# Reading two DRAM-bounced tiles by rows of 16 or 32 partitions instead of by columns of 96, with the opening's requests reordered

## The chip, the cores and the metric

The kernel runs on one core of a Trainium2 chip. The metric is the device time of one launch in microseconds, as the median of several executions. A profiled execution of the same program gives the trace; its times are counted from the first instruction. "Span" is the time from the first to the last instruction in that trace, and the launch's own time is a little longer than the span.

The engines are named as the profile does: PE (matrix multiplies), PEld (weight loads for PE), DVE (vector), ACT (scalar), POOL (GpSimd) and SP (which here only issues DMA requests). SPq is SP's queue of requests.

## The reference, cut to what matters

Eight sequences of 3008 tokens with 256 channels go through a spectral layer, and the result through a two-layer expert with ELU:

```
X  = rfft(x, axis=1)                       # x: [8, 3008, 256]
Yr = Xr @ w_r - Xi @ w_i + b_r             # 256 x 256 weights
Yi = Xr @ w_i + Xi @ w_r + b_i
Yr, Yi = soft threshold by 0.01
y  = irfft(Yr + i Yi, n=3008)              # [8, 3008, 256]
h  = y @ moe_w_in                          # 256 x 2048
g  = where(h > 0, h, exp(min(h, 0)) - 1)
out = g @ moe_w_out                        # 2048 x 256
```

## The kernel before, in words

**The transform.** 3008 is 47 times 64, and each transform is done in two matrix steps with a trip through DRAM between them, because the second step contracts over another index than the first. For one batch the units are:

- A (6 units, `unit_A`): the transform over 64 samples. Each unit multiplies four of 24 column groups of the loaded input by the table `M1`, copies the result to SBUF as `A`, and writes it to the DRAM tile `DA` of shape [24 (j), 128, 256].
- Z: `load_Z` reads `DA` back with another split of its indices. The partitions of `Z` are (j, half, real or imaginary), 96 in all; the free dimension has 32 columns (s) of 256 channels, 16 KB for each partition in bf16.
- X (8 units, `unit_X`): the transform over 47, one small matmul for each column s, contracting over all 96 partitions of `Z`. Unit u uses columns 8(u//2) to 8(u//2)+7.
- M (12 groups, `unit_M` or in the opening `first_M`): the 256 x 256 complex weights, bias and soft threshold.
- B (6 units, `unit_B`): the inverse transform over 64, written to the DRAM tile `DB` of shape [24 (k), 128, 256].
- Bs: `load_Bs` reads `DB` back with 96 partitions (k, real or imaginary, half) and 32 columns, as `Z` is read.
- Y (8 units, `unit_Y`): the inverse transform over 47, contracting over all 96 partitions of `Bs`; unit u uses columns 8(u//2) to 8(u//2)+7.

**The expert.** All tokens are cut into blocks of 512, each block into 8 steps of 256 hidden columns. `front` multiplies by the scaled input weights and starts the exponential, `elu` and `finish_elu` complete it, and `back` multiplies by the output weights two steps later. One batch is 47 such steps, about 2.3 us each.

**What sets the order.** The program is written out by hand (`manual_schedule`): each engine executes its instructions in the order of the program text, and a DMA request waits on the queue of the engine that issues it, with everything that stands behind it. SP issues nearly all requests: writes of `DA` and `DB`, reads of `Z` and `Bs`, the weights and the output. POOL issues the reads of x and of the output weights. From batch 1 on, the transform of the next batch is spread over the expert steps of the current one by `plan` (f0: units ahead of the step's `front`; f1: requests after it). Batch 0 has nothing to hide behind: its transform is the opening, about 57 us, in which `idle_pe(n)` puts n matmuls without use into PE's queue to keep it running.

**The opening, in order.** Tables on DVE, ACT and POOL; six A units with a `DA` write each (line 155); the requests for w_r and w_i (518, 519); four reads of `Z`, eight columns each (164); 40 idle matmuls (562); X; M and B interleaved, with a `DB` write after each B (260); two reads of `Bs` (271); the six A units of batch 1 (each followed by two idle matmuls) with two more reads of `Bs` among them; then Y and the expert steps. The reads of `Z` and `Bs` can only start once all six writes have landed, since each column has parts of all of them; the first X unit needs only the first read of `Z`, the first Y unit only the first read of `Bs`.

Of the kernel before, what the change touches and what calls it, by code (L numbers as in the profile page):

```python
# [29 lines left out]
def kernel(  # L30
# [46 lines left out]
    dram = ctx.enter_context(tc.tile_pool(name="dram", bufs=2, space=bass.MemoryType.DRAM))  # L77
    zp = ctx.enter_context(tc.tile_pool(name="zp", bufs=1))
    wk2 = ctx.enter_context(tc.tile_pool(name="wk2", bufs=2))
    wk3 = ctx.enter_context(tc.tile_pool(name="wk3", bufs=3))  # L80
    wk4 = ctx.enter_context(tc.tile_pool(name="wk4", bufs=4))
    xtp = ctx.enter_context(tc.tile_pool(name="xtp", bufs=1))
# [46 lines left out]
    def unit_A(b, u, alone=False, on_dve=False, ahead=False):  # L129
        ci, uu = u // 2, u % 2  # L130
        if uu == 0:
            if ahead and ci > 0:
                A_of[b, ci] = late3.tile([P, 8, D], BF16, name="A", tag="gT")
            elif alone:
                A_of[b, ci] = wk4.tile([P, 8, D], BF16, name="A", tag="Bs")
# [5 lines left out]
        dav = DA_of[b].rearrange("j p d -> p j d")  # L141
# [6 lines left out]
        evac(  # L148
            A[:, 4 * uu : 4 * uu + 4, :].rearrange("p n d -> p (n d)"),
            ps[:].rearrange("p a b -> p (a b)"), on_dve,  # L150
        )
        j0 = 8 * ci
        if alone:
            j0 += 4 * uu
            nc.sync.dma_start(dav[:, j0 : j0 + 4, :], A[:, 4 * uu : 4 * uu + 4, :])
        elif uu == 1:
            nc.sync.dma_start(dav[:, j0 : j0 + 8, :], A[:])

    def load_Z(b, s0, s1):

        if b not in Z_of:
            Z_of[b] = zp.tile([2 * NR, NS, D], BF16, name="Z", tag="Z")
        dv = DA_of[b].rearrange("j (h c s) d -> (j h c) s d", h=2, c=2)
        nc.sync.dma_start(Z_of[b][:, s0:s1, :], dv[:, s0:s1, :])

# [100 lines left out]

    def load_Bs(b, w):

        Bs = wk4.tile([4 * K1, 8, D], BF16, name="Bs", tag="Bs")
        dv = DB_of[b].rearrange("k (c h m) d -> (k c h) m d", c=2, h=2)  # L270
        nc.sync.dma_start(Bs[:], dv[:, 8 * w : 8 * w + 8, :])
        Bs_of[b, w] = Bs

    def unit_Y(b, u, alone=False, on_dve=False):
        w, dt = u // 2, u % 2
        if u == 0:
            yT_of[b] = late2.tile([P, 2, S], BF16, name="yT", tag="yT")
        yT, Bs = yT_of[b], Bs_of[b, w]
        ps = unit_ps("yps", alone)
        psv = ps[:].rearrange("p a (k j) -> p (a k) j", j=P)  # L280
        for j in range(8):
            nc.tensor.matmul(  # L282
                psv[:, j, 0 : 2 * N1], lhsT=Bs[:, j, dt * P : dt * P + P], rhs=M4[:],
                start=True, stop=True,
            )
# [9 lines left out]
    def idle_pe(n):  # L295

        for _ in range(n):
            nc.tensor.matmul(ips[:], lhsT=busy[:, 0:P], rhs=busy[:], start=True, stop=True)

    brow, rest = (wk3.tile([P, 2 * D], F32, name="yb", tag="yb") for _ in range(2))  # L300
    nc.vector.memset(brow[:], 0.0)
    for o, bv in ((0, b_r), (D, b_i)):
        for k in range(3):
            nc.sync.dma_start(
                brow[32 * k : 32 * k + 1, o : o + D],
                bass.AP(tensor=bv.tensor, offset=bv.offset, ap=[[0, 1], [1, D]]),
            )
    idle_pe(9)
    xts = []
    for ci in range(3):  # L310
        xt = constp.tile([P, 8, D], F32R, name=f"xt{ci}")
        xts.append(xt)
    with tc.tile_pool(name="stagep", bufs=1) as stagep:
# [202 lines left out]
        signs(0)  # L516
        fA(5)
        nc.sync.dma_start(w_r_f[:], w_r.rearrange("(c p) e -> p c e", p=P))
# [42 lines left out]
        )  # L561
        idle_pe(40)

# [9 lines left out]
    def load_w_in(q):  # L573
        if q < 3:
# [9 lines left out]

    def gate(src):

        t = gatep.tile([P, 1], F32, name="gate", tag="gate")
        nc.gpsimd.tensor_copy(t[0 : src.shape[0], :], src)


    def fB(v, on_dve=False):
        unit_B(0, v, alone=True, on_dve=on_dve)

    load_w_in(0)
    gate(Z_of[0][:, 8, 0:1])
    for ci in range(3):
        load_x(1, ci)
    load_w_out(0)
    nc.vector.tensor_scalar(w3[:], v3[:], CMAGIC, -CMAGIC, ALU.add, ALU.add)
    nc.vector.tensor_tensor(w3[:], v3[:], w3[:], ALU.subtract)  # L600
    nc.scalar.copy(bias_p[:], brow[:])
    nc.vector.tensor_tensor(rest[:], brow[:], bias_p[:], ALU.subtract)
    for u in range(8):
        unit_X(0, u, alone=True, on_dve=u in (1, 4, 7))
        if u == 1:
            nc.scalar.activation(a3[:], w3[:], AF.Abs)
            nc.vector.tensor_copy(bias_p[32:64], rest[32:64])
            nc.vector.tensor_copy(bias_p[64:P], rest[64:P])
            nc.vector.tensor_tensor(rest[64:P], rest[64:P], bias_p[64:P], ALU.subtract)
            nc.vector.tensor_copy(bias_p[64:P], rest[64:P])  # L610
        idle_pe(1)
    for o, src, sc, bi in ((1, w3, TURN, 0.0), (0, a3, -TURN, hpi[:])):
# [12 lines left out]
    first_M(1, 0, False)  # L625
    nc.scalar.activation(r4[:], v4[:], AF.Sin, bias=0.0, scale=TURN)
    nc.scalar.activation(dume[:], busy[:, 0:1], AF.Exp, scale=0.0)
# [24 lines left out]
    load_Bs(0, 0)  # L652
    load_Bs(0, 1)

# [6 lines left out]

    scale_w_in(0, True)
    for u in range(6):
        unit_A(1, u, on_dve=bool(u % 2), ahead=True)
        if u == 1:
            scale_w_in(1, True)
            for w in (2, 3):
                load_Bs(0, w)
            gate(Bs_of[0, 2][:, 0, 0:1])
            load_w_out(1)  # L670
            load_w_in(3)
# [128 lines left out]
    def plan(b):  # L800
# [18 lines left out]
        for t, u in enumerate(seq, lead):  # L819
# [7 lines left out]
            else:  # L827
                f0[t].append(put(u[0], n1, *u[1:]))
            if u == ("A", 1):
                f1[t] += [(load_Bs, (n1, w)) for w in range(4)]  # L830
            if u == ("A", 5) and n2 < B:
                f1[t] += [(load_Z, (n2, s0, s1)) for s0, s1 in ((0, 8), (8, NS))]
        if b == 0:
            f1[3].append((scale_w_in, (3, True, 0)))
            f1[4].append((scale_w_in, (3, True, 1)))
            f1[xs[0]].append((lambda: gate(Z_of[1][:, 16, 0:1]), ()))
        if n2 < B:
# [61 lines left out]
```

## Time and profile before

| | |
|---|---|
| median of 3 runs | 912.49 us (911.72 to 914.93) |
| the profiled execution's own time | 911.36 us |
| its span | 909.6 us |
| PE busy | 893.2 us (98%) |
| DVE, ACT, POOL busy | 79%, 77%, 35% of the span |
| bytes moved by DMA | 106.24 MB, 117 GB/s on average |

The share of PE is an average. From about 60 us on PE is continuously fed; the opening is where PE's work is partly idle matmuls and waits. A line of the timeline gives start and length in us, the engine, the line of the code, the operation and, in brackets, the idle time before it and what ended it. A line of the windows gives a stretch, the busy time of each engine with the number of instructions, and at its end the clock granted to PE (1.00 is full), the busy share of the 16 DMA engines and the rate in GB/s.

### The profile page before, as it was taken

What the parts mean: (1) busy time and instruction counts of PE and PEld (TensorE: products, weight loads), DVE (VectorE), ACT (ScalarE), POOL (GpSimd) and SP (SyncE); (2) the same over time, 40 slices, a digit from 0 to 9 for tenths busy, and PEclk for the clock granted to TensorE, in tenths of its full rate; (3) what the DMA queues carried; (4) which work ended last, traced back from release to release, by engine and by line L of the source; (5) the groups of instructions that cost most, each with busy time, mean ns of one, the idle gap of its engine ahead of it and who ended that gap; (6) DMA issues with size and microseconds to landing.
All of it is one profiled execution on the core that took longest, in us unless ns stands there. A gap on an engine that the chain in (4) does not pass through costs nothing.

```text
span 909.6 us, 17270 instructions
## 1 busy us (share of the span) xinstructions
PE 893.2 (98%) x6721; PEld 652.3 (72%) x6721; DVE 717.5 (79%) x891; ACT 696.8 (77%) x850; POOL 314.9 (35%) x438
## 2 busy tenths in 40 slices
PE   8989999999999999999999999999999999999997
PEld 3447667876688667886678766787667866777775
DVE  8669778887788778897788877888778877778776
ACT  6768788777878778787787888778887877767664
POOL 6701540333321441405404153033332134443664
PEclk9999999999999999999999999999999999999999
DMA  8997116721283215732166032752228111231011
GB/s 270 309 269 228 47 48 186 209 70 47 77 241 124 71 47 143 190 109 85 56 201 194 24 99 59 217 161 72 69 72 230 30 42 47 82 82 48 24 48 46
DMA packets 90670, 106.24 MB, mean 117 GB/s; under 512 B 5270, under 2 KB 81308, under 8 KB 87228
## 3 DMA queue, kind: packets, MB, share of 16 engines
q1 hardware_dynamic: 84332, 77.62, 30.6%
q0 software_dynamic: 5968, 27.26, 9.1%
q8 instruction: 52, 0.85, 0.4%
q10 hardware_dynamic: 288, 0.26, 0.1%
q14 instruction: 30, 0.25, 0.1%
HBM read 55.32 MB, written 49.81 MB: 116 GB/s over the span
## 4 chain that ended last, share of the span: by engine, by line
PE 85%; DVE 5%; ACT 3%; DMA 3%; issue 2%; POOL 1%; SPq 1%; DVEq 0%; ACTq 0%; POOLq 0%
PE ps_o L773 34%; PE hps L715 34%; PE mps L192 9%; PE yps L282 2%; PE bps L244 2%; PE xps L175 2%; PE aps L144 2%; DMA Bs<-DB 2%; DVE gT L742 1%; DVE Et L754 1%; ACT Et L729 1%; ACT Et L726 1%; DMA xt<-in_x_dram 1%; DVE osb L784 1%; ACT Bz L257 1%
## 5 line engine op out<-in xcount | busy, mean ns | idle before, releaser
L773 PE MATMUL ps_o<-w_out_r,gT 128*128 128x256 f32 x3008 | 477.0, 301 | 0.2 <-DVE gT L740 0.2
L773 PEld LDWEIGHTS ps_o<-w_out_r,gT 128*128 128x128 f32 x3008 | 403.4, 189 | 50.3 <-DVE osb L784 1.3
L715 PE MATMUL hps<-yT,w_in_s 128*128 128x512 bf16 (+4 forms) x1728 | 389.9, 353 | 2.5 <-DVE gT L742 1.2
L740 DVE SCALAR_TENSOR_TENSOR gT<-Et,hps 128x512 fp32r<-128x512 f32 (+1 forms) x272 | 222.8, 848 | 75.3 <-POOL Et L752 38.2
L742 DVE SCALAR_TENSOR_TENSOR gT<-hps,Et 128x1024 fp32r<-128x1024 f32 x198 | 242.2, 1223 | 16.5 <-PE ps_o L773 1.0
L715 PEld LDWEIGHTS <-w_in_s 128*128 128x128 bf16 x1728 | 141.6, 98 | 129.4 <-issue 23.0
L729 ACT ACTIVATE Et<-hps 128x1024 f32<-128x1024 f32 x198 | 204.0, 1030 | 13.2 <-PE hps L715 6.7
L752 POOL TENSOR_SCALAR Et<-Et 128x512 f32<-128x512 f32 x187 | 111.4, 615 | 222.9 <-ACT Et L724 222.9
L754 DVE TENSOR_SCALAR Et<-Et 128x1024 f32<-128x1024 f32 x198 | 137.0, 692 | 48.0 <-ACT Et L729 40.1
L210 POOL TENSOR_SCALAR clip<-yb 128x512 f32<-128x512 f32 x84 | 51.7, 615 | 316.0 <-DVE yb L202 278.6
L724 ACT ACTIVATE Et<-hps 128x512 f32<-128x512 f32 x188 | 102.1, 595 | 63.9 <-PE hps L715 63.9
L726 ACT ACTIVATE Et<-hps 128x1024 f32<-128x1024 f32 x84 | 86.3, 1027 | 71.5 <-PE hps L715 71.0
L211 POOL TENSOR_TENSOR Y<-yb,clip 128x512 bf16<-128x512 f32 x84 | 107.2, 1276 | 7.0
L727 ACT ACTIVATE Et<-Et 128x1024 f32<-128x1024 f32 x84 | 88.8, 1058 | 2.7
L202 DVE TENSOR_TENSOR yb<-mps,bias_bc 128x512 f32<-128x512 f32 x89 | 61.4, 689 | 35.4 <-PE mps L192 28.6
L127 ACT CAST XT<-xps 128x768 bf16<-128x768 f32 x61 | 48.8, 800 | 15.8 <-PE xps L175 15.8
L127 ACT CAST yT<-yps 128x752 bf16<-128x752 f32 x63 | 49.7, 788 | 14.2 <-PE yps L282 14.1
L192 PE MATMUL mps<-wcat_r,XT 128*128 128x512 bf16 x192 | 58.2, 384 | 0.8 <-ACT Bz L257 0.3
L127 ACT CAST A<-aps 128x1024 bf16<-128x1024 f32 x45 | 45.6, 1014 | 15.3 <-PE aps L144 13.8
L192 PE MATMUL mps<-wcat_s,XT 128*128 128x512 bf16 x192 | 57.1, 379 | 0.0
L192 PEld LDWEIGHTS <-XT 128*128 128x128 bf16 x384 | 30.8, 98 | 29.6 <-DVE XT L125 0.6
L257 ACT CAST Bz<-bps 128x1024 bf16<-128x1024 f32 x46 | 46.0, 1000 | 2.5 <-PE bps L244 2.5
(110 smaller groups left out, 412.9 us busy)
## 6 DMA issues: line engine op xcount, KB each, us to landing
xt<-in_x_dram POOLq DMA_DIRECT2D x21, 1024.0 KB, 7.1
out_dram<-osb SPq DMA_DIRECT2D x158, 128.0 KB
Bs<-DB SPq DMA_DIRECT2D x32, 384.0 KB
DA<-A SPq DMA_DIRECT2D x21, 512.0 KB
DB<-Bz SPq DMA_DIRECT2D x21, 512.0 KB
Z<-DA SPq DMA_DIRECT2D x7, 1152.0 KB
Z<-DA SPq DMA_DIRECT2D x11, 384.0 KB
xt<-in_x_dram POOLq DMA_DIRECT2D x6, 512.0 KB, 5.9
```

The lines of the kernel that those rows point to most:

```text
L127: nc.scalar.copy(dst, src)
L192: nc.tensor.matmul(ps, lhsT=XT[:, dt, c, o : o + P], rhs=wm[:, dt, :], start=(not biased and m == 0 and dt == 0), stop=(m == 1 and dt == 1),)
L211: nc.gpsimd.tensor_tensor(Y_of[b, q][:, i, :], yb, clip[:], ALU.subtract)
L715: nc.tensor.matmul(hps[:, s, c0:c1], lhsT=w_in_s[:, dt, ft * P : ft * P + P], rhs=yT_of[b][:, dt, t0 : t0 + c1 - c0], start=(dt == 0), sto ...
L724: nc.scalar.activation(E_[:, s], hps[:, s], AF.Exp)
L726: nc.scalar.activation(E_, hps[:], AF.Relu, scale=-1.0)
L729: nc.scalar.activation(E_, hps[:], AF.Exp)
L740: nc.vector.scalar_tensor_tensor(o, e, -1.0, h, ALU.add, ALU.max)
L742: nc.vector.scalar_tensor_tensor(o, h, 0.0, e, ALU.max, ALU.add)
L752: eng.tensor_scalar(E_[:, s], E_[:, s], 1.0, 0.0, ALU.min, ALU.max)
L754: nc.vector.tensor_scalar(E_, E_, 1.0, -1.0, ALU.min, ALU.add)
L773: nc.tensor.matmul(po[q][:, i_ % 2, :], lhsT=gT[:, s, i_ * P : i_ * P + P], rhs=w_out_r[:, ft, :], start=(ft == 0 and i_ % 2 == 0), stop=( ...
```

## The change

`Z` and `Bs` are read by rows: one request reads all 32 columns (16 KB) of the partitions that one written unit fills. In the opening that is 16 partitions (256 KB) for each unit, six requests for each tile, each issued as soon as the write of its own unit has landed. In the later batches it is 32 partitions (512 KB) after every second unit, three requests for each tile. `Bs` becomes one tile of the same total size as its four former buffers, so the later batches' reads of `Bs` are placed after the last Y unit of the batch before.

Beside this the opening is reordered. The w_r and w_i requests stand after the reads of `Z`; the four casts of w_r and w_i go from POOL to DVE, between X units; the rounding of the table argument `w3` goes from DVE to POOL; `a3` goes behind X; the sine of `r4` goes ahead of X; the load of the exponential's table (`dume`) goes from the M phase to after the last B unit; the x requests of batch 1 are held until w_i has landed. The split of the bias into three bf16 parts is done on a [128, 4] tile on POOL and brought into its row form through a small DRAM tile, in place of six one-row requests and work on 512-wide rows on ACT and DVE. Of the input weights, part 2 is requested later and scaled on DVE in the first expert steps instead of on ACT; part 1 is requested later. Three idle matmuls fewer stand ahead of X.

```diff
-    def load_Z(b, s0, s1):
+    def load_Z(b, j0, j1):
...
-        dv = DA_of[b].rearrange("j (h c s) d -> (j h c) s d", h=2, c=2)
-        nc.sync.dma_start(Z_of[b][:, s0:s1, :], dv[:, s0:s1, :])
+        dv = DA_of[b][j0:j1].rearrange("j (h c s) d -> (j h c) s d", h=2, c=2)
+        nc.sync.dma_start(Z_of[b][4 * j0 : 4 * j1], dv)
...
-    def load_Bs(b, w):
-
-        Bs = wk4.tile([4 * K1, 8, D], BF16, name="Bs", tag="Bs")
-        dv = DB_of[b].rearrange("k (c h m) d -> (k c h) m d", c=2, h=2)
-        nc.sync.dma_start(Bs[:], dv[:, 8 * w : 8 * w + 8, :])
-        Bs_of[b, w] = Bs
+    def load_Bs(b, k0, k1):
+        if b not in Bs_of:
+            Bs_of[b] = bsp.tile([P, NS, D], BF16, name="Bs", tag="Bs")
+        dv = DB_of[b][k0:k1].rearrange("k (c h m) d -> (k c h) m d", c=2, h=2)
+        nc.sync.dma_start(Bs_of[b][4 * k0 : 4 * k1], dv)
...
+        for u in range(6):
+            load_Z(0, 4 * u, 4 * u + 4)
         nc.sync.dma_start(w_r_f[:], w_r.rearrange("(c p) e -> p c e", p=P))
         nc.sync.dma_start(w_i_f[:], w_i.rearrange("(c p) e -> p c e", p=P))
-        pool.tensor_copy(wcat_r[:, :, 0:D], w_r_f[:])
-        pool.tensor_copy(wcat_r[:, :, D : 2 * D], w_i_f[:])
-        pool.tensor_scalar(wcat_s[:, :, 0:D], w_i_f[:], -1.0, None, ALU.mult)
-        pool.tensor_copy(wcat_s[:, :, D : 2 * D], w_r_f[:])
-        for g in range(4):
-            load_Z(0, 8 * g, 8 * g + 8)
+        nc.sync.dma_start(bd[:], bp3[:])
...
-        idle_pe(40)
+        nc.scalar.activation(r4[:], v4[:], AF.Sin, bias=0.0, scale=TURN)
+        pool.tensor_scalar(w3[:], v3[:], CMAGIC, -CMAGIC, ALU.add, ALU.add)
+        pool.tensor_tensor(w3[:], v3[:], w3[:], ALU.subtract)
+        idle_pe(37)
...
+        for u in range(8):
+            unit_X(0, u, alone=True, on_dve=u in (1, 4, 7))
+            if u in (1, 4):
+                for dst, src, sc in casts[u // 2 : u // 2 + 2]:
+                    dve.tensor_scalar(dst, src[:], sc, None, ALU.mult)
+            if u == 0:
+                t = stagep.tile([P, 1], F32, name="gate")
+                pool.tensor_copy(t[:], w_i_f[:, 1, D - 1 : D])
+                for ci in range(3):
+                    load_x(1, ci)
+            idle_pe(1)
...
     fB(0)
-    load_w_in(1)
...
     fB(1)
+    load_Bs(0, 0, 4)
...
     fB(2)
+    load_Bs(0, 4, 8)
+    load_w_in(1)
...
     fB(3)
-    load_w_in(2)
+    load_Bs(0, 8, 12)
...
     fB(4)
+    load_Bs(0, 12, 16)
     idle_pe(3)
     fB(5, True)
+    load_Bs(0, 16, 20)
+    load_Bs(0, 20, 24)
+    load_w_in(2)
+    nc.scalar.activation(dume[:], busy[:, 0:1], AF.Exp, scale=0.0)
...
-    load_Bs(0, 0)
-    load_Bs(0, 1)
...
-            for w in (2, 3):
-                load_Bs(0, w)
...
-    scale_w_in(2, False)
-    for s0, s1 in ((0, 8), (8, NS)):
-        load_Z(1, s0, s1)
+    load_w_in(3)
+    for ci in range(3):
+        load_Z(1, 8 * ci, 8 * ci + 8)
...
-            if u == ("A", 1):
-                f1[t] += [(load_Bs, (n1, w)) for w in range(4)]
-            if u == ("A", 5) and n2 < B:
-                f1[t] += [(load_Z, (n2, s0, s1)) for s0, s1 in ((0, 8), (8, NS))]
+            if u[0] == "B" and u[1] % 2:
+                at_ = max(t, seq.index(("y", 7)) + lead) + 1
+                f1[at_].append((load_Bs, (n1, 4 * u[1] - 4, 4 * u[1] + 4)))
+            if u[0] == "A" and u[1] % 2 and n2 < B:
+                f1[t + (u[1] < 5)].append((load_Z, (n2, 4 * u[1] - 4, 4 * u[1] + 4)))
         if b == 0:
-            f1[3].append((scale_w_in, (3, True, 0)))
-            f1[4].append((scale_w_in, (3, True, 1)))
+            for t in range(4):
+                f1[t + 1].append((scale_w_in, (2 + t // 2, True, t % 2)))
```

More of the change, by code (lines that the diff above doesn't have):

```diff
@@ L78 @@
     zp = ctx.enter_context(tc.tile_pool(name="zp", bufs=1))
+    bsp = ctx.enter_context(tc.tile_pool(name="bsp", bufs=1))
     wk2 = ctx.enter_context(tc.tile_pool(name="wk2", bufs=2))
     wk3 = ctx.enter_context(tc.tile_pool(name="wk3", bufs=3))
-    wk4 = ctx.enter_context(tc.tile_pool(name="wk4", bufs=4))
     xtp = ctx.enter_context(tc.tile_pool(name="xtp", bufs=1))
@@ L134, in unit_A @@
             elif alone:
-                A_of[b, ci] = wk4.tile([P, 8, D], BF16, name="A", tag="Bs")
+                if ci == 0:
+                    A_of[b, "all"] = bsp.tile([P, NS, D], BF16, name="A", tag="Bs")
+                A_of[b, ci] = A_of[b, "all"][:, 8 * ci : 8 * ci + 8, :]
             else:
@@ L140, in unit_A @@
         xt, A = xts[ci], A_of[b, ci]
-        dav = DA_of[b].rearrange("j p d -> p j d")
         ps = unit_ps("aps", alone or ahead)
@@ L151, in unit_A, with write_A @@
         )
+        if not ahead:
+            write_A(b, u, alone)
+    def write_A(b, u, alone=False):
+        ci, uu = u // 2, u % 2
+        A, dav = A_of[b, ci], DA_of[b].rearrange("j p d -> p j d")
         j0 = 8 * ci
@@ L277, in unit_Y @@
             yT_of[b] = late2.tile([P, 2, S], BF16, name="yT", tag="yT")
-        yT, Bs = yT_of[b], Bs_of[b, w]
+        yT, Bs = yT_of[b], Bs_of[b]
         ps = unit_ps("yps", alone)
@@ L282, in unit_Y @@
             nc.tensor.matmul(
-                psv[:, j, 0 : 2 * N1], lhsT=Bs[:, j, dt * P : dt * P + P], rhs=M4[:],
+                psv[:, j, 0 : 2 * N1],
+                lhsT=Bs[0 : 4 * K1, 8 * w + j, dt * P : dt * P + P], rhs=M4[:],
                 start=True, stop=True,
@@ L298, in idle_pe @@
             nc.tensor.matmul(ips[:], lhsT=busy[:, 0:P], rhs=busy[:], start=True, stop=True)
[L300 to L307, printed above, removed]
-    idle_pe(9)
+    idle_pe(9)
+    b4 = constp.tile([P, 4], F32, name="b4")
+    bp3 = constp.tile([P, 3, 4], BF16, name="bp3")
+    for o, bv in ((0, b_r), (P // 2, b_i)):
+        nc.sync.dma_start(b4[o : o + P // 2, :], bv.rearrange("(p j) -> p j", j=4))
+    bd = dram.tile([P, 3, 4], BF16, name="bd", tag="bd")
+    nc.vector.memset(bias_p[:], 0.0)
     xts = []
@@ L498 @@
         pool.tensor_tensor(v4[:], v4[:], r4[:], ALU.subtract)
+        for k in range(3):
+            pool.tensor_copy(bp3[:, k, :], b4[:])
+            if k < 2:
+                pool.tensor_tensor(b4[:], b4[:], bp3[:, k, :], ALU.subtract)
         def fA(u):
@@ L561 @@
         )
-        idle_pe(40)
+        nc.scalar.activation(r4[:], v4[:], AF.Sin, bias=0.0, scale=TURN)
+        pool.tensor_scalar(w3[:], v3[:], CMAGIC, -CMAGIC, ALU.add, ALU.add)
+        pool.tensor_tensor(w3[:], v3[:], w3[:], ALU.subtract)
+        idle_pe(37)
+        casts = (
+            (wcat_r[:, :, 0:D], w_r_f, 1.0), (wcat_r[:, :, D : 2 * D], w_i_f, 1.0),
+            (wcat_s[:, :, 0:D], w_i_f, -1.0), (wcat_s[:, :, D : 2 * D], w_r_f, 1.0),
+        )
+        for u in range(8):
[9 more added lines that the diff above has]
+            idle_pe(1)
     gatep = ctx.enter_context(tc.tile_pool(name="gatep", bufs=2))
@@ L573, in load_w_in @@
     def load_w_in(q):
-        if q < 3:
+        if q < 2:
             wf = late3.tile([P, 2, FQ], F32, name="w_in_f", tag="Et")
@@ L583, in load_w_out, with gate @@
         nc.gpsimd.dma_start(w_out_r[:, hf, :], w_out_v[:, hf, :])
-    def gate(src):
+    def gate(tile_, p0, p1, s):
         t = gatep.tile([P, 1], F32, name="gate", tag="gate")
-        nc.gpsimd.tensor_copy(t[0 : src.shape[0], :], src)
+        nc.gpsimd.tensor_copy(t[p0:p1, :], tile_[p0:p1, s, 0:1])
     def fB(v, on_dve=False):
         unit_B(0, v, alone=True, on_dve=on_dve)
+    nc.sync.dma_start(bias_p[0:3, :].rearrange("k (p j) -> k p j", j=4), bd.rearrange("p k j -> k p j"))
     load_w_in(0)
-    gate(Z_of[0][:, 8, 0:1])
-    for ci in range(3):
-        load_x(1, ci)
     load_w_out(0)
[L599 to L611, printed above, removed]
+    nc.scalar.activation(a3[:], w3[:], AF.Abs)
     for o, src, sc, bi in ((1, w3, TURN, 0.0), (0, a3, -TURN, hpi[:])):
@@ L625 @@
     first_M(1, 0, False)
-    nc.scalar.activation(r4[:], v4[:], AF.Sin, bias=0.0, scale=TURN)
-    nc.scalar.activation(dume[:], busy[:, 0:1], AF.Exp, scale=0.0)
     first_M(1, 1, True)
@@ L662 @@
     scale_w_in(0, True)
+    gate(Bs_of[0], 64, 4 * K1, 0)
+    load_w_out(1)
     for u in range(6):
         unit_A(1, u, on_dve=bool(u % 2), ahead=True)
+        if u % 2:
+            write_A(1, u)
         if u == 1:
             scale_w_in(1, True)
-            for w in (2, 3):
-                load_Bs(0, w)
-            gate(Bs_of[0, 2][:, 0, 0:1])
-            load_w_out(1)
-            load_w_in(3)
         idle_pe(2)
-    scale_w_in(2, False)
-    for s0, s1 in ((0, 8), (8, NS)):
-        load_Z(1, s0, s1)
+    load_w_in(3)
+    for ci in range(3):
+        load_Z(1, 8 * ci, 8 * ci + 8)
     idle_pe(3)
@@ L828, in plan @@
                 f0[t].append(put(u[0], n1, *u[1:]))
[L829 to L832 removed]
+            if u[0] == "B" and u[1] % 2:
[3 more added lines that the diff above has]
+                f1[t + (u[1] < 5)].append((load_Z, (n2, 4 * u[1] - 4, 4 * u[1] + 4)))
         if b == 0:
[L834 to L836 removed]
+            for t in range(4):
+                f1[t + 1].append((scale_w_in, (2 + t // 2, True, t % 2)))
+            f1[xs[0]].append((lambda: gate(Z_of[1], 64, 2 * NR, 0), ()))
         if n2 < B:
```

## The prediction, made before the changed kernel ran

> **What bounds the kernel now.** I read the page's shares first, then the waits of PE and SP, then the opening's timeline queue by queue, and last the windows for DMA rates. PE is busy 98% of the span, and after 60 us it waits 4 us in all. Only the opening, where PE's work is partly idle matmuls, can move much. There the path runs through two trips to DRAM.
>
> ```profile
> PE 893.2 (98%) x6721; PEld 652.3 (72%) x6721; DVE 717.5 (79%) x891; ACT 696.8 (77%) x850; POOL 314.9 (35%) x438
> PE yps L282 <- DMA Bs<-DB: 2.9, 3, 1.0
> SPq L164 <- DMA DA<-A: 37.1, 10, 9.3
> ```
>
> The second line: units Y waited three times for `Bs`, 1.0 us at worst. The third: SP stood before reads of `Z` for writes of `DA`. The timeline of SP, PE and ACT in the opening:
>
> ```profile
> 15.66 0.50 SPq L518 DMA_DIRECT2D w_r_f<-in_w_r_dram  x1
> 18.40 1.74 SPq L164 DMA_DIRECT2D Z<-DA  x4
> 14.01 8.81 PE L298 MATMUL ips<-busy 128*128 128x512 bf16 x40
> 23.25 0.51 PE L175 MATMUL xps<-M,Z 96*128 96x96 bf16 x8 [0.43 <-DMA Z<-DA]
> 30.50 0.39 PE L192 MATMUL mps<-wcat_r,XT 128*128 128x512 bf16 x1 [0.33 <-DVE XT L125]
> 55.16 0.84 PE L282 MATMUL yps<-M,Bs 96*128 96x94 bf16 x16 [1.01 <-DMA Bs<-DB]
> 33.26 1.28 ACT L627 ACT_TABLE_LOAD   x1
> ```
>
> The last A write lands at 18.40, X starts at 23.25 after the fills (end 22.82) and a wait of 0.43, M at 30.50, Y at 55.16. The chain shows the second trip:
>
> ```profile
> 48.19 2.77 DMA DB<-A
> 51.15 3.97 DMA Bs<-DB
> ```
>
> Two windows give the rate of narrow and of full-width reads, with the DMA engines busy in both (share above 1): reads of 96 partitions (`Z`) moved 262 GB/s, reads of 128 partitions (x and weights) 426. The next two show the clock after PE's work thinned out at 54 us.
>
> ```profile
> 24.00:25.00 1.00, 0.81 (x15) 0.49 (x13) 1.00 (x2) 1.00 (x2) 1.00 (x2) 1.00 1.04 262
> 33.00:34.00 1.00, 1.00 (x7) 0.43 (x5) 0.70 (x2) 0.99 (x3) 0.92 (x2) 1.00 1.07 426
> 57.50:58.00 0.50, 0.50 (x4) 0.22 (x3) 0.00 (x0) 0.00 (x0) 0.00 (x0) 0.50 1.16 311
> 58.00:59.00 1.00, 1.00 (x11) 0.72 (x10) 0.00 (x0) 0.87 (x1) 0.00 (x0) 0.50 1.02 254
> ```
>
> **The price of a narrow read.** No read of 16 partitions is in the trace. 256 KB at the 96-partition rate (262) is 1.0 us. If the rate goes with the partitions reached, 426 x 16/128 = 53 GB/s, it is 4.9 us. From 128 to 96 partitions the rate fell by 38%, more than the 25% fewer partitions, so narrowness does cost; but these rows are four times as long. Between ends a factor five apart I take the geometric middle, 2.2 us. Six requests on one queue follow one another: 13.2 us of transfer for `Z` in place of 5.9 (1.5 MB at 262).
>
> [...]
>
> **Z and X.** The first request is issued where w_r's stood, 15.66. Fixed time around a transfer: the `DB` write took 2.77 us, of which 256 KB at 426 is 0.6, so 2.15. X contracts over all rows, so it waits for the sixth: 15.66 + 2.15 + 13.2 = 31.0, against 23.25: +7.75. The three fills removed (8.81/40 = 0.22 each) end PE's cover at 22.15; that gains nothing here. From X to M it took 7.25 us, with waits for `Z` and with `a3` (0.85 us) among ACT's copies. With all of `Z` there, the copies set the pace (ACT 0.81, DVE 0.97 through two PSUM buffers): eight units end 6.3 us after the start, -0.95. But PE has then stood for 8.9 us; the rows at 57.5 show half clock after a thinner stretch, which lasted until about 60.9, 3.4 us. Between nothing and half of two such stretches I take +1.0. `a3` and two sines (0.85, 0.85, 0.92) now follow X on ACT, so DVE's first adds of M come 0.8 to 1.1 us later beside PE; three PSUM buffers cover half: +0.4 (0 to 0.8). M is at 8.2 us later than before.
>
> **What else moves there, at nothing.** Four casts of w (POOL: 2.11, 0.93, 2.20, 0.60) become four on DVE (0.42 each by line 658's half-width form) between X copies, when DVE otherwise waits for PE; the w requests follow `Z` in the queue and land about 2 us after it, when the first cast is due; if later, DVE holds back X unit 4. The rounding (DVE 0.85 and 1.25) goes to POOL, about 2.8 us, done long before `a3`. The bias: two 64-row requests for six of one row; ACT loses 0.60 and DVE 3.2 us; POOL gets five operations of 128x4 in its idle 6.0 us before 19.87; the two requests through DRAM are done some 4 us before the first biased M (31.15 before, 39 now). The memset is no longer than the one removed. x of batch 1 is requested about 7 us later, as is the unit that needs it. The r4 sine (0.23) moves into ACT's idle 2.1 us ahead of X.
>
> **Bs and Y.** In the clock of before (all shifted by the 8.2): the first row read goes behind the second `DB` write, at 40.9, moving from 42.2. From there SP's queue carries, in order, six reads at 2.2, among them four `DB` writes at 0.6 and 512 KB of w_in at 1.2 (both at 426): 16.8 us, to 59.0, and 1.0 to land: 60. Each read waits on SP for its write and holds back the next write behind it; followed one by one it is 60.2. The first Y needs the last read: +5.0 against 55.16. The exponential's table (1.28 and 0.20), now behind the last B, delays the copy of the first A unit and PE's third by 0.9; the A units end at 55.05 in place of 54.15, all under that wait. The half clock at 57.4 was there before; a longer stand adds +0.5 (0 to 1.7). Part 2 of w_in is requested behind the last read, lands 1.2 us after it and is scaled in steps 1 and 2, before step 4 uses it; ACT loses 1.06, DVE gets two scalings of 0.42 in steps where PE already waited for DVE: +0.2 (0 to 0.8).
>
> **Later batches.** 512 KB on 32 partitions: 2.0 us at 262, 4.9 in proportion, middle 3.1. The last read is issued in the same step as before; the earlier two are long done. In five of seven batches about 8 us lie between request and use (249.58 to 258.27), which hides it. In the other two (143.24 to 149.35 and 793.41 to 797.83) Y waited 0.9 and 1.0; the first read there was 384 KB, 1.5 us, but ran beside three more. I add +1.0 in all (-1 to +3). `Z` requests go between other work of SP, whose waits for `DA` (some 3 us each) hold up output writes; the next X is more than 20 us away.
>
> **Sum.** 7.75 - 0.95 + 1.0 + 0.4 + 5.0 + 0.5 + 0.2 + 1.0 = +14.9 on the profiled 911.4: 926.3. That execution lies 1.1 under the median shown, within the runs' spread; I say 926.
>
> **Rivals.** *Narrow reads run at the wide rate, and it is faster.* For it: each engine moves a 16 KB row, four times as long a piece as now. Against: the fall from 426 to 262. Then `Z`'s last read, issued at 18.4, lands at 18.4 + 2.15 + 1.0 = 21.6, X starts when the fills end, 22.2 (-1.05), and -0.95 and +0.4 follow: -1.6. The last `Bs` lands at 51.2 + 3.15 = 54.4, before the A units end at 55.05: no gain at Y, but without the 1.0 us stand the clock may stay up, half of 3.4 us more: -1.6 to -3.3, 908 to 910. It decides from below 1.1 us for a request; above, the queue begins to outlast the fills and the A units.
>
> *Reads of different partitions run side by side.* Then only the last of six shows: X at 18.4 + 2.15 + 2.2 = 22.75 (25.5 with 4.9), Y at 51.2 + 2.15 + 2.2 = 55.6: with the small terms -1 to +4, 910 to 915. Against it: the four reads of `Z` now in one queue land one after another, the first and the third X unit waiting 0.43 and 0.19 us for the first and the second of them. [...]
>
> *The change doesn't do what it says*, a row read still waiting for all six writes: in the built program each waits for its own unit's write alone, so I give it nothing.
>
> **How the numbers follow.** Slow narrow reads, 0.60, with a range of their own of 917 to 935 (1.5 to 2.8 us for a request, about 12 us of time for each us of request). Wide rate, 0.27, of which 0.17 beyond 0.3%. Side by side, 0.13: 0.01 faster, 0.07 same, 0.05 slower. 0.3%, 2.7 us, is about what a measurement of this kernel can tell from no change. So faster 0.18, same 0.17, slower 0.65. From 909 to 933 leaves out about 0.1 at each end.
>
> **What would show it.** X's first matmul at 31 with a wait for `Z` near 9 us (22.2 with none by the first rival); windows of reads alone with a DMA share near 1 and 100 to 130 GB/s; a wait of about 5 us before the first Y; PE clock 0.50 in X. Wrong if narrow reads move above 200 GB/s, or if the clock or the w casts cost more than given.

## The result and the profile after

The changed kernel takes 935.64 us (median of six runs, 932.62 to 940.9) against 912.38 (911.72 to 914.93): the ratio is 1.0257, with a 95% interval of 1.0216 to 1.0298. The prediction was 926, from 909 to 933. The direction was right; the loss was 23 us and not 14, and the median lies 2.6 us beyond the range.

The profiled execution took 940.9 us, its span 939.1. First the busy line of its page and the longest waits of PE (waited for: us in total, times, longest):

```profile
PE 906.1 (96%) x6718; PEld 661.3 (70%) x6718; DVE 713.5 (76%) x890; ACT 695.9 (74%) x848; POOL 312.4 (33%) x441
PE xps L182 <- DMA Z<-DA: 9.8, 1, 9.8
PE yps L289 <- DMA Bs<-DB: 5.1, 2, 4.5
PE mps L196 <- DMA bias_p<-bd: 3.3, 1, 3.3
PE ps_o L786 <- DMA w_out_r<-in_moe_w_out_dram: 1.7, 1, 1.7
```

PE's share fell from 98% to 96%, and four waits make it: for `Z`, for `Bs`, and two that the prediction did not have, for the bias and for the second half of w_out. The span is 29.5 us longer than before; in 16.6 of them PE is idle (33.0 us in place of 16.4), and in the other 12.9 it is busy, so matmuls that take longer carry nearly half of the loss. The timeline of PE puts three of the waits in their place:

```profile
32.16 0.80 PE L182 MATMUL xps<-M,Z 96*128 96x96 bf16 x8 [9.80 <-DMA Z<-DA]
40.41 0.39 PE L199 MATMUL mps<-wcat_r,XT 128*128 128x512 bf16 x1 [0.36 <-DVE XT L125]
44.51 0.59 PE L196 MATMUL mps<-bias_p,busy 128*128 128x512 bf16 x1 [3.28 <-DMA bias_p<-bd]
74.85 1.29 PE L289 MATMUL yps<-M,Bs 96*128 96x94 bf16 x16 [4.53 <-DMA Bs<-DB]
```

The chain of work that ended last runs through DMAs for most of the opening (start, length, what):

```profile
16.48 5.53 DMA Z<-DA
22.07 11.52 DMA bd<-bp
33.64 10.83 DMA bias_p<-bd
65.63 4.87 DMA DB<-A
70.56 4.20 DMA Bs<-DB
75.44 18.73 DMA w_out_r<-in_moe_w_out_dram
```

The bias' write (3 KB) stands behind `Z` and the two w requests in its queue and lands 11.52 us after its issue; the read back, again 3 KB, takes 10.83. The windows show the `Z` reads by themselves (PE, PEld, DVE, ACT, POOL; then PE's clock, DMA share, GB/s):

```profile
23.00:24.00 1.00, 0.00 (x0) 0.00 (x0) 0.00 (x0) 0.00 (x0) 1.00 (x1) 1.00 1.87 229
24.00:25.00 1.00, 0.00 (x0) 0.00 (x0) 0.00 (x0) 0.00 (x0) 1.00 (x1) 1.00 0.13 16
25.00:26.00 1.00, 0.00 (x0) 0.00 (x0) 0.00 (x0) 0.00 (x0) 0.92 (x2) 1.00 2.01 246
26.00:27.00 1.00, 0.00 (x0) 0.00 (x0) 0.00 (x0) 0.00 (x0) 1.00 (x1) 1.00 0.13 16
...
29.00:30.00 1.00, 0.00 (x0) 0.00 (x0) 0.00 (x0) 0.00 (x0) 0.00 (x0) 0.50 0.44 40
```

The packets of a request are put down to the window in which they begin, so a request shows in two windows: 127 GB/s on average, 2.1 us for 256 KB. And PE's clock is at 0.50 when X begins.

The opening explains only part of the loss. One further difference is in every later batch. The matmuls of the output weights, by shape, from 183 to 700 us (busy, mean ns of one), before:

```profile
L773 PE MATMUL ps_o<-w_out_r,gT 128*128 128x256 f32 x1790 | 283.9, 301 | 0.0
```

and after:

```profile
L786 PE MATMUL ps_o<-w_out_r,gT 128*128 128x256 f32 x1784 | 286.3, 303 | 0.0
```

Two ns more for each of 3008 matmuls are 6 us, though the change touches neither their code nor their inputs. In the same stretch the bf16 matmuls of before and after agree to 1 ns (`hps` 380 in both at 128x512, `mps` 384 and 379 in both, `xps` 208 and 207, `yps` 210, `bps` 272).

The marks of the opening by start of PE's work, with the prediction's sum beside them. The column "933.3" is the unaltered changed kernel in an execution that had no wait for the bias (a_again, below):

| us | before, 911.4 | after, 940.9 | after, 933.3 | 933.3 less before | predicted |
|---|---|---|---|---|---|
| first X | 23.25 | 32.16 | 32.34 | +9.1 | +7.75 |
| M's second matmul | 30.50 | 40.41 | 40.03 | +9.5 | +8.2 |
| last B | 46.15 | 61.07 | 55.97 | +9.8 | +8.2 |
| end of batch 1's A units and their idle matmuls | 54.15 | 70.32 | 65.23 | +11.1 | +9.1 |
| first Y | 55.16 | 74.85 | 69.83 | +14.7 | +13.2 |
| X of batch 1 | 72.77 | 95.28 | 89.28 | +16.5 | +13.9 |
| X of batch 7 | 716.28 | 744.17 | 736.62 | +20.3 | +14.9 |
| end of the span | 909.6 | 939.1 | 931.5 | +21.9 | +14.9 |

### The profile page after: what moved, and what is told of

Read it like the earlier page. It is cut to its first block, busy times and chain, and to the rows that moved or that the text cites. A ratio compares the mean times of both kernels' runs of the same rounds, so it can differ in the third digit from the quotient of the medians.

```text
span 939.1 us, 17264 instructions
## 1 busy us (share of the span) xinstructions
PE 906.1 (96%) x6718; PEld 661.3 (70%) x6718; DVE 713.5 (76%) x890; ACT 695.9 (74%) x848; POOL 312.4 (33%) x441
## 4 chain that ended last, share of the span: by engine, by line
PE 86%; DMA 7%; ACT 2%; DVE 2%; issue 1%; SPq 0%; POOL 0%; DVEq 0%; ACTq 0%; POOLq 0%
PE ps_o L786 35%; PE hps L728 33%; PE mps L199 9%; PE bps L251 2%; PE yps L289 2%; PE xps L182 2%; DMA w_out_r<-in_moe_w_out_dram 2%; PE aps L145 2%; DMA bd<-bp 1%; DMA bias_p<-bd 1%; DMA Bs<-DB 1%; ACT Et L739 1%; ACT Bz L264 1%; DMA Z<-DA 1%; DMA DB<-A 1%
## 5 line engine op out<-in xcount | busy, mean ns | idle before, releaser
L786 PE MATMUL ps_o<-w_out_r,gT 128*128 128x256 f32 x3008 | 484.0, 303 | 1.9 <-DMA w_out_r<-in_moe_w_out_dram 1.7
L786 PEld LDWEIGHTS ps_o<-w_out_r,gT 128*128 128x128 f32 x3008 | 408.5, 189 | 52.4 <-DMA w_out_r<-in_moe_w_out_dram 2.2
L127 ACT CAST A<-aps 128x1024 bf16<-128x1024 f32 x45 | 45.5, 1013 | 16.3 <-PE aps L145 15.1
## 6 DMA issues: line engine op xcount, KB each, us to landing
w_out_r<-in_moe_w_out_dram POOLq DMA_DIRECT2D x2, 1024.0 KB, 16.4
```

What stands on the lines that cost most here:

```text
L127: nc.scalar.copy(dst, src)
L786: nc.tensor.matmul(po[q][:, i_ % 2, :], lhsT=gT[:, s, i_ * P : i_ * P + P], rhs=w_out_r[:, ft, :], start=(ft == 0 and i_ % 2 == 0), stop=( ...
```

## The experiments

**The changed kernel again, and three parts undone.** The first is the changed kernel as it is, to see which of its marks move from one execution to another.

> The changed kernel once more, unaltered. Its six times fell in two groups, 932.6 to 933.0 and 938.3 to 940.9, and the profiled one (940.9) had steps of the later batches 0.7% longer (2.165 us against 2.147). If that belongs to the execution and not to the kernel: some executions near 932.8 again, and in a profile of such a one the shift against the kernel before stays near 20 to 22 us from batch 1 to the end. If the row reads slow the later batches: the shift grows by 0.8 us in each batch here too.

It took 935.55 us (933.3 to 940.72; ratio 1.0263, 1.0227 to 1.0299). Its times, like those of the result, lie in two clusters, 932.6 to 934 and 937 to 941. The profile of the 933.3 has no wait for the bias at all. In the view of DMAs of the 940.9, from 34 to 37 us and from 37 to 45:

```profile
DMA packets 382, 0.51 MB, mean 170 GB/s; under 512 B 320, under 2 KB 320, under 8 KB 320
...
DMA packets 725, 3.11 MB, mean 389 GB/s; under 512 B 114, under 2 KB 230, under 8 KB 403
```

and of the 933.3, the same stretches:

```profile
DMA packets 448, 0.50 MB, mean 168 GB/s; under 512 B 387, under 2 KB 387, under 8 KB 387
...
DMA packets 714, 3.21 MB, mean 401 GB/s; under 512 B 48, under 2 KB 183, under 8 KB 391
```

The read of `bias_p` consists of 384 pieces of 8 bytes. In the 933.3 they are all through by 37 us; in the 940.9 some 65 of them are left then (114 small packets against 48), and come while x is read, 389 GB/s in all; M waits for the last until 44.5. So there is a race between this read and the reads of x, and the issue times agree. In the 933.3 the bias read goes out 0.32 us ahead of the first x request (33.48 and 33.80) and is never waited for; in the 940.9 it goes out 0.05 us ahead (33.64 and 33.69), and M waits 3.3 us. The shift grows after batch 1's X in both, by 3.8 us to batch 7's X in the 933.3 and by 5.4 in the 940.9. The 1.5 between them lie right behind the wait for w_out, where the clock of the 940.9 falls to 0.50 once more (96 to 98 us) and that of the 933.3 does not.

Next, both tiles by columns in all batches, requested where the kernel before had them, with the rest of the change kept:

```diff
-        dv = DA_of[b][j0:j1].rearrange("j (h c s) d -> (j h c) s d", h=2, c=2)
-        nc.sync.dma_start(Z_of[b][4 * j0 : 4 * j1], dv)
+        dv = DA_of[b].rearrange("j (h c s) d -> (j h c) s d", h=2, c=2)
+        nc.sync.dma_start(Z_of[b][:, s0:s1, :], dv[:, s0:s1, :])
...
-        nc.sync.dma_start(Bs_of[b][4 * k0 : 4 * k1], dv)
+        nc.sync.dma_start(Bs_of[b][0 : 4 * K1, k0:k1, :], dv[:, k0:k1, :])
```

> The changed kernel with both tiles read by columns again, in the opening and later; the reordering of the opening stays. Theory (the 16-partition reads carry the loss): X starts at 23 to 24 in place of 32.2, the wait before the first Y falls from 4.5 to about 1, PE keeps its clock in X; 914 to 919, with whatever the bias path costs by itself left in. Rival (the reordering carries it: bias through DRAM, later x and weights): above 925.

923.6 us (923.41 to 928.57; ratio 1.0137, 1.011 to 1.0165). Both sides missed: on the medians the rows cost 12 us in this company (10 between the lower times, 933.3 and 923.4), and the reorder alone costs 11. X begins at 23.60, but M at 32.67, since DVE stands 3.2 us for w_r among its X copies; and PE waits 4.5 us in the first steps for `gT`, which DVE writes late, behind its waits for w_in and for writes of `DA`. The spacing of the batches stayed at that of the changed kernel (727.2 - 80.34 = 646.9 us from batch 1's X to batch 7's, 647.3 in a_again, 643.5 before). So up to batch 7's X the row reads of the later batches cost half a us. In the last batch the first Y unit of a_again stands 1.50 us, where that of a_cols waits 0.63. The view names no releaser; the unit needs all three row reads, the last one too:

```profile
818.84 0.49 PE L289 MATMUL yps<-M,Bs 96*128 96x94 bf16 x8 [1.50 <-issue]
```

From batch 1's X to the end of the span it is 842.2 us in a_again, 841.3 in a_cols and 836.8 before: 1.0 us for the rows, and the growing shift is not theirs.

Then the bias' trip ahead of the reads of x:

```diff
+        nc.sync.dma_start(bd[:], bp3[:])
         for u in range(6):
             load_Z(0, 4 * u, 4 * u + 4)
...
+        nc.sync.dma_start(bias_p[0:3, :].rearrange("k (p j) -> k p j", j=4), bd.rearrange("p k j -> k p j"))
         sines(0, 0)
```

> The changed kernel with the bias's two requests earlier: the write to DRAM ahead of the row reads of Z, the read back behind the bias_bc requests, no longer beside the x and w_out reads. Theory (the wait of 3.3 us before the second M group and the half clock behind it are this read's): 4 to 5 us less than the changed kernel, the wait gone. Rival (the read is slow by itself, or as late behind the row reads): within 1.5 us of the changed kernel.

932.66 us (931.99 to 935.18; ratio 1.0231, 1.021 to 1.0252). No wait for the bias, and no upper cluster in its four executions: 3 us off the median, nearly all of it from the upper cluster, where 4 to 5 were expected. Against the lower cluster little is gained.

Last of these, the row reads with the 16 partitions of one request six apart, not side by side; the tables are permuted to fit:

```diff
-        nc.sync.dma_start(Z_of[b][4 * j0 : 4 * j1], dv)
+        for q in range(j0 // 4, j1 // 4):
+            o = 16 * q - 4 * j0
+            nc.sync.dma_start(Z_of[b][q : 2 * NR : 6], dv[o : o + 16])
```

> The changed kernel with each 16-row read put on partitions 6 apart (u, u+6, ... u+90) in place of 16 neighbours, in all batches; the tables' columns are permuted alike, some ten one-column operations on DVE more. Same bytes, rows, engines and order. [...] Rival (a read of 16 rows of 16 KB is slow as such): packets stay at 2.1 us and the time within 2 us of the changed kernel's.

924.49 us (923.17 to 925.13; ratio 1.0132, 1.0117 to 1.0147), half a us above the author's 917 to 924, which had `Z` landed by 24 to 26. The same bytes in the same rows and order, and X begins at 25.71:

```profile
PE xps L184 <- DMA Z<-DA: 3.8, 1, 3.8
PE yps L293 <- DMA Bs<-DB: 1.7, 2, 1.3
```

From the issue of the first read (15.47) and with the 2.15 us of fixed time taken off, a request took (25.71 - 15.47 - 2.15)/6 = 1.35 us; in the changed kernel it is (32.16 - 16.48 - 2.15)/6 = 2.26. The view of DMAs of a_spread from 20 to 23 us, while `Z` is read:

```profile
DMA packets 92, 0.75 MB, mean 251 GB/s; under 512 B 46, under 2 KB 46, under 8 KB 46
```

That is about the rate of the column reads (262) and twice the 127 of the changed kernel. What was slow is the neighbourhood of the partitions, neither their number nor the rows.

**The later batches.** The change adds two small tiles, `b4` and `bp3`. By the sizes and the order of the tiles in the program (no trace shows addresses) they take 32 bytes each in every partition, so all tiles behind them move by 64 bytes; `gT`, which PE loads as weights for the output matmuls, moves from a 128-byte boundary to the middle between two. One run makes the move 128 bytes in the changed kernel, and one moves the tiles by 64 bytes in the kernel before:

```diff
-    b4 = constp.tile([P, 4], F32, name="b4")
+    b4 = constp.tile([P, 24], F32, name="b4")[:, 0:4]
```

> The changed kernel with one small tile made 64 bytes longer, so that every later tile lies 128 bytes behind its place in the kernel before instead of 64; instructions and their order are unchanged. Theory, a tile that starts off a 128-byte boundary makes PE's matmuls with gT slower: the matmuls of the output weights take 301 ns in place of 303, a batch takes 108.15 us in place of 108.84, and the whole 928 to 931 (about 5 to 6 us less). Rival, the rest of the reorder slows the later batches: 303 ns and 933 to 936 as before this edit.

```diff
     idle_pe(9)
+    gap = constp.tile([P, 16], F32, name="gap")
+    nc.gpsimd.memset(gap[:, 0:1], 0.0)
```

> The kernel before with nothing but an unused tile of 64 bytes ahead of xt, which moves every later tile by 64 bytes. Theory of the 128-byte boundary: the matmuls of the output weights go from 301 to 303 ns, and the time to 916 to 918 (5 to 6 us more). Rival: 912, nothing changes.

The first: 934.45 us (930.65 to 938.67; ratio 1.0225, 1.018 to 1.027), in the two clusters of the bias race, of which the lower lies some 2 us below that of a_again, less than the 5 to 6 expected. Its median says little, but its matmuls are back, and from batch 1's X to batch 7's it takes 645.0 us, where all nine runs with 303 ns take 646.8 to 648.9:

```profile
L786 PE MATMUL ps_o<-w_out_r,gT 128*128 128x256 f32 x1785 | 284.0, 301 | 0.0
```

The second is clear: 916.99 us (916.8 to 918.13), 4.5 more than before; the ratio is 1.0045 (1.003 to 1.006). A tile that no matmul reads costs half a per cent here. Which tile's place it is, one more run tells, with a gap that moves `gT` alone:

```diff
     load_w_in(0)
+    gap = late3.tile([P, 16], F32, name='gap', tag='gap')
+    nc.gpsimd.memset(gap[:, 0:1], 0.0)
```

> The kernel before with an unused tile placed so that gT alone starts 64 bytes past a 128-byte boundary (xt, Et, w_out_r and the rest stay where they were). Theory, it is gT, which PE reads as weights, whose place costs: the matmuls of the output weights take 303 ns in place of 301, those of A units with xt stay at 395, and the time is 915 to 917. Rival, it takes another tile (Et, osb or xt), so 301 ns and 912 to 913.

918.19 us (916.83 to 919.47; ratio 1.0062, 1.0048 to 1.0076):

```profile
L775 PE MATMUL ps_o<-w_out_r,gT 128*128 128x256 f32 x1772 | 285.3, 303 | 0.0
```

It is `gT`. (The A units' mean was 398 ns here, 397 with everything shifted and 395 before, though xt did not move; it doesn't follow the place of xt.)

**What the reorder costs.** From the run by columns on, its parts were undone one after another: first the w requests back ahead of `Z`, then w_in, w_out and the table of the exponential back in their old places.

```diff
+        nc.sync.dma_start(w_r_f[:], w_r.rearrange("(c p) e -> p c e", p=P))
+        nc.sync.dma_start(w_i_f[:], w_i.rearrange("(c p) e -> p c e", p=P))
         for g in range(4):
             load_Z(0, 8 * g, 8 * g + 8)
-        nc.sync.dma_start(w_r_f[:], w_r.rearrange("(c p) e -> p c e", p=P))
-        nc.sync.dma_start(w_i_f[:], w_i.rearrange("(c p) e -> p c e", p=P))
```

> The changed kernel with both tiles read by columns, and the requests for w_r and w_i put ahead of those for Z again. Theory: in the run by columns DVE stood 3.2 us for w_r and that put M 1.8 us later; with w there early M comes at 30.5 to 31 in place of 32.7, and the time is 921 to 922 in place of 923.6. Rival, the time between X and M is set by ACT's copies and not by the casts: M stays above 32 and the time within 0.7 us of 923.6.

```diff
     first_M(1, 0, False)
+    nc.scalar.activation(dume[:], busy[:, 0:1], AF.Exp, scale=0.0)
...
     fB(0)
+    load_w_in(1)
...
     fB(3)
+    load_w_in(2)
...
+            load_w_out(1)
+            load_w_in(3)
         idle_pe(2)
+    scale_w_in(2, False)
```

> As the run before, and the input weights w_in, the second half of w_out and the table of the exponential are requested and scaled where the kernel before had them. Theory, the rest of the reorder's cost in the opening is the late w_in that holds DVE in the first steps and keeps back gT: batch 1's X comes at 73 to 74 in place of 80.3 and the time is 916 to 918, of which 5 to 6 us over the kernel before is the shift by 64 bytes. Rival, the rest lies elsewhere in the reorder (the bias through DRAM, a3 behind X): 920 to 922.

Both failed by far: 933.96 us (933.6 to 934.42; ratio 1.0229, 1.0213 to 1.0244) and 929.97 (929.55 to 930.21; 1.0184, 1.0169 to 1.0199), 10 and 6 more than with the w requests late. Between the two, w_in, w_out and the table in their old places are worth 4.0 us (PE waits 1.9 us for `gT` and not 6.6). M did come earlier (29.82), but then, in the first of them:

```profile
41.58 0.59 PE L196 MATMUL mps<-bias_p,busy 128*128 128x512 bf16 x1 [10.94 <-DMA bias_p<-bd]
```

The reads of x are held until w_i has landed. With w early, x's 3 MB are requested at 26.44, the bias read at 27.64, and it loses the race outright: 13.9 us for 3 KB. In the changed kernel the late w kept x back to 33.7, and the race was an even one: five of the ten executions of after and a_again lie in the lower cluster.

So the bias' trip was put ahead of x here too, and the gap of 64 bytes closed, which leaves of the change the bias on a small tile, the casts on DVE, the rounding on POOL and the order of three sines. Relative to the run before:

```diff
-    b4 = constp.tile([P, 4], F32, name="b4")
+    b4 = constp.tile([P, 24], F32, name="b4")[:, 0:4]
...
+        nc.sync.dma_start(bd[:], bp3[:])
         for g in range(4):
...
+        nc.sync.dma_start(bias_p[0:3, :].rearrange("k (p j) -> k p j", j=4), bd.rearrange("p k j -> k p j"))
```

> Both tiles by columns, w, w_in, w_out and the exponential's table requested where the kernel before had them, the bias' trip through DRAM put ahead of the reads of x (write before the reads of Z, read right after the requests of bias_bc), and the 128-byte shift. What is left of the change is the bias on a 128x4 tile, the casts on DVE, the rounding on POOL, a3 behind X and the r4 sine ahead of it. Theory, the reorder cost only by the late w, the late w_in, the shift and the bias read that meets the reads of x: no wait for the bias, M at 30 to 31, 910 to 914. Rival, something else of the reorder costs: over 916.

914.59 us (913.6 to 915.59; ratio 1.0016, 1.0007 to 1.0026), just over the 910 to 914 expected and 1.5 us over the kernel before, which took 913.09 beside it. There is no wait for the bias, but M comes at 32.42 and not at 30 to 31. The 15.4 us between the two runs are the bias wait (11.3 in the run before, none here) and the shift (4.5). X begins 1.6 us later than in the kernel before, with the bias' write now ahead of `Z` in the queue; that is about the size of what is left, though no run takes it alone. Of the reorder's 11.4 us (923.6 against 912.2) the shift has 4.5, w_in and its company 4.0, and 1.5 are left in c_all; the other 1.4 would be the late w's, which put M 1.8 us later, but no run shows that by itself.

**The rows, one tile at a time.** On this cleared ground each tile was read by rows of 16 partitions in the opening alone:

```diff
-        for g in range(4):
-            load_Z(0, 8 * g, 8 * g + 8)
+        for u in range(6):
+            rows_Z(0, 4 * u, 4 * u + 4)
```

> The run c_all with nothing but the opening's Z read by rows of 16 partitions. Theory, six requests of 2.1 us: X at 31 to 32.5 in place of 23, and 8 to 10 us more than c_all. Rival, the rows alone cost little and it was their company with the w requests: under 5 us.

```diff
     fB(1)
+    rows_Bs(0, 0, 4)
...
     fB(2)
+    rows_Bs(0, 4, 8)
...
     fB(5, True)
+    rows_Bs(0, 16, 20)
+    rows_Bs(0, 20, 24)
```

> The run c_all with nothing but the opening's Bs read by rows of 16 partitions, each behind its own write. Theory: Y waits 4 to 5 us for the last read, and the whole is 3 to 6 us more than c_all. Rival, Bs has slack without the delay of the rest: within 1 us of c_all.

`Z`: 922.42 us (920.91 to 923.37; ratio 1.0101, 1.0086 to 1.0117), 7.8 more than c_all; X moves from 24.83 to 32.78. `Bs`: 921.47 (920.94 to 922.02; 1.0091, 1.0074 to 1.0107), 6.9 more; Y moves from 57.76 to 64.71. The first is just under what was expected, the second costs more than the 3 to 6 us expected. The wait for `Z` in the first, then those for `Bs` in the second:

```profile
PE xps L188 <- DMA Z<-DA: 10.7, 1, 10.7
```

```profile
PE yps L295 <- DMA Bs<-DB: 8.5, 3, 7.5
```

That makes 14.7 us if the two add up. For `Z`, a_spread puts most of it down to the partitions being neighbours. For `Bs` it is less plain, and three runs tried rows on spread partitions. The first takes c_all and reads `Bs` alone so:

```diff
+    rows_Bs(0, 0, 4)
...
-                f1[t] += [(load_Bs, (n1, 8 * w, 8 * w + 8)) for w in range(4)]
+                f1[t] += [(rows_Bs, (n1, 0, 24))]
```

> The run c_all with Bs read by rows, those of one request put on partitions six apart, in all batches (the tables of Y are permuted to fit). Theory, some 1.1 us for a request: the last lands at about 54.4 in place of Bs' column reads, Y waits under 0.5 us, and the time is 0 to 3 us less than c_all, so that it may come below the kernel before. Rival, six more requests on the queue with its waits hold w_in and the writes back: 1 us or more over c_all.

949.58 us (948.94 to 950.1; ratio 1.04, 1.0385 to 1.0416). This edit spoiled its own ground: the permuted table's columns were put on POOL ahead of the bias' split, so the bias' write went out at 22.44 and the four `Z` reads behind it on SP after that; X began at 28.68, M waited 7.7 us for the bias again (its read, though 0.8 us ahead of x, had `Z` still ahead of it), and six requests in one step of each later batch made Y wait five times, 15.1 us in all. It decides nothing between its theories. The next takes the kernel before and changes the opening's `Bs` alone, with the later batches still read by columns:

```diff
     fB(1)
+    rows_Bs(0)
...
-    load_Bs(0, 0)
-    load_Bs(0, 1)
+    rows_Bs(4)
+    rows_Bs(5)
```

> The kernel before with one thing taken from the change in another form: in the opening Bs is read by rows on partitions six apart, each behind its own write; later batches read by columns into the same order of partitions. Theory, the last 256 KB land 1.0 to 1.5 us earlier than the column reads, Y waits under 0.5 us for them, and the time is 910 to 912, 0.5 to 2 us less than before. Rival, w_in among the reads and the waits of SP cost as much as is saved or more: 912 to 916.

916.91 us (916.22 to 917.93; ratio 1.0045, 1.0032 to 1.0059): the rival's upper end and a little more. The last B is where it was (46.27 against 46.15), but SP shows what the rows do to the writes:

```profile
47.94 0.51 SPq L284 DMA_DIRECT2D Bs<-DB  x1
48.54 0.53 SPq L262 DMA_DIRECT2D DB<-Bz  x1
49.20 0.49 SPq L284 DMA_DIRECT2D Bs<-DB  x1
49.74 0.58 SPq L605 DMA_DIRECT2D w_in_f<-in_moe_w_in_dram  x1
50.41 0.44 SPq L262 DMA_DIRECT2D DB<-A  x1
51.85 0.50 SPq L284 DMA_DIRECT2D Bs<-DB  x1
52.44 0.53 SPq L262 DMA_DIRECT2D DB<-A  x1
56.53 1.86 SPq L284 DMA_DIRECT2D Bs<-DB  x2
```

A read waits on SP until its write has landed, and the next write waits behind the read: the last `DB` write goes out at 52.44 where it was 48.19, and the chain has it landing 5.44 us later, where that took 2.77. Y begins at 61.43 instead of 55.16. So with w_in among them, early reads on the writes' own queue lose 6 us even when their partitions are far apart. In the changed kernel's order, with part 2 of w_in behind the reads, spreading did cut the wait for `Bs` from 4.6 (a_again) to 1.3. How the 6.9 us divide between queue and rate depends on what else stands in that queue, and these runs don't divide it further.

The last run mends the changed kernel in all points at once:

```diff
+            nc.sync.dma_start(Z_of[b][q : 2 * NR : 6], dv[o : o + 16])
...
+    b4 = constp.tile([P, 24], F32, name="b4")[:, 0:4]
...
+        nc.sync.dma_start(w_r_f[:], w_r.rearrange("(c p) e -> p c e", p=P))
+        nc.sync.dma_start(w_i_f[:], w_i.rearrange("(c p) e -> p c e", p=P))
+        nc.sync.dma_start(bd[:], bp3[:])
         for u in range(6):
             load_Z(0, 4 * u, 4 * u + 4)
```

> The changed kernel, rows and all, with its side costs removed: the rows of one request on partitions six apart, the 128-byte shift, the bias' trip ahead of the reads of x, w, w_in, w_out and the table where the kernel before had them. Theory, the parts add up: c_all's 914.6, some 1 us for X (1.1 us for a request) and up to 2 for Y, 914 to 918. Rival, the parts meet again on SP's queue: over 919.

921.62 us (920.17 to 922.25; ratio 1.0097, 1.0084 to 1.0111). The parts meet again: with w and the bias ahead of them, the six reads of `Z` are issued from 18.07 instead of 15.47, and X begins at 28.8. Y waits only 1.1 us, but everything up to the first Y stands 3.4 to 4.0 us later than in c_all, and X of batch 1 stands 5.5 us later, behind waits of 2.6 us for a copy of Y and 1.7 for `gT`. Against c_rows_z, whose X began at 32.78, spreading the partitions got back half of what the rows of `Z` had cost there. No version here beats the kernel before; c_all comes nearest.

## Why the prediction was wrong, point by point

Two steps failed, and a third was too small. One is the paragraph that put the rest of the reorder "at nothing": it priced two requests of 3 KB by their size, and they cost 2 to 3 us on the median. The other is the step on later batches: it counted only waits for `Bs`, +1.0, and 5.4 us were lost there, nearly all by where `gT` lies.

**The price of a narrow read** was right in size: 2.2 us was taken, and 2.26 (in the 940.9) and 2.37 (in the 933.3) came out. It was the middle of two bounds a factor of five apart, so that it fits is in part luck. The prediction put the price down to narrowness, that is, to few partitions. Sixteen partitions six apart are as few, and a_spread read them at 251 GB/s where neighbours gave 127, so it is their place and not their number. The two rivals with cheap reads fell: X waited 9.8 us. Why neighbours are slower, no run here shows.

**Z and X** was right: +8.2 predicted, +9.5 at M's second matmul in the 933.3, and 7.8 us of time when `Z` was tested alone. The difference lies ahead of X: there the first read was issued at 15.95 and not at 15.66, and six requests at (32.34 - 15.95 - 2.15)/6 = 2.37 us and not 2.2 make 1.0 us more. From X to M it took 7.7 us, as the sum has it (7.25 - 0.95 + 1.0 + 0.4), and the half clock in X is there (0.50 from 28 to 37 us in the 940.9).

**Bs and Y** was right: +5.0 predicted, and in the 933.3 execution Y moved 14.7 - 9.8 = 4.9 us further than the last B. The account of the queue, each read holding back the next write, is what b_spread_b shows. The A units lost 1.3 us for 0.9, but lay under the wait as said. Alone, on c_all, it cost 6.9.

**Later batches** failed. The step counted only Y's waits for `Bs` and gave them 1.0 us more; in the 933.3 they are 2.1 us (0.62 and 1.50) where they were 1.9, so that this part was about right. What it left out is where tiles lie: the two new small tiles moved `gT` by 64 bytes, 2 ns on each of 3008 matmuls, 4.5 us by b_shift and 5.5 by b_gT. In the trace of before nothing shows this; but that the change adds two small tiles was to be seen in its text, and the step gave that no price.

**"What else moves there, at nothing"** failed in two places. The sentence that "the two requests through DRAM are done some 4 us before the first biased M" priced the bias by its size. In the 940.9 the write landed 11.52 us after its issue, behind `Z` and w on its queue, and the read took 10.83 beside x, so that M stood 3.3 us, with half clock for some 3.4 us behind it; the last B came 5.1 us later than in the 933.3. That is two thirds of the 7.6 us between these two executions. Of the rest, 1.0 came by batch 1's X and 1.5 with the second half clock behind the wait for w_out. How its 384 pieces and the company of x made a read of 3 KB that long, no run here shows. The work put under cover had its cover, but the step named none for two transfers that queue behind 1.5 MB and beside 3 MB. The same paragraph let the w requests follow `Z` "about 2 us after it"; by rows this did hold, because X was late as well, and by columns it cost DVE 3.2 us.

**Half clock at Y and part 2 of w_in** (+0.5 and +0.2) were too small: between the first Y and batch 1's X the 933.3 execution lost 1.8 us more. Its chain passes through the second half of w_out, now requested only when the last `Bs` has landed, and PE waits 1.4 us for it, more than the 1.1 that the two terms lack. The prediction did not follow that request.

**The sum.** Against the 933.3 execution the misses are 1.3 to the second M, 0.2 more to the first Y, 1.1 to batch 1's X, and 4.4 from there to the end (5.4 lost where 1.0 was given), which is nearly all the shift of `gT`: 7.0 in all. On the median lie 2 to 3 us of the bias race besides. Of the 10 us that were missing, 1.5 lie in the two steps that the change is named for.

## What to carry to other kernels

A reordering that "moves nothing but requests" has to be followed request by request: a 3 KB read in 8-byte pieces took 11 to 19 us from issue to landing when it met a bulk read, and PE never waited for it when it was issued well ahead (at 22.64 in c_all, where M comes at 32.42). Compare where the tiles lie before and after a change: here 64 bytes ahead of the fp32 tile that PE loads as weights cost half a per cent. And reads that wait for their own queue's writes should not stand ahead of the next write; in b_spread_b, with w_in among them, that cost 6 us at the first Y.

## What the runs showed of the hardware that was not expected

The matmuls with fp32 weights from `gT` take 301 ns when the tile starts on a 128-byte boundary, by the layout that follows from the program, and 303 when it starts 64 bytes behind one (300 or 301 in the eight runs of the first kind, 303 in the nine of the second). With 2.15 us of fixed time taken off, an estimate from the `DB` write of before, 16 neighbouring partitions take 256 KB in 2.26 us (in the 940.9), 16 partitions six apart in 1.35 (a_spread). And one kernel can have two times by its own doing: the changed kernel's executions lie in two clusters, 3 to 8 us apart, and in the profiled ones it is whether 384 pieces of 8 bytes slip through before x's packets that parts them; with two requests moved there was one cluster.
